# A gated mix of attention and a gated feed-forward: the first eight key tiles in one round, sixteen scores among the last projection units, and the first loads in another order

## The chip, the core and the metric

The kernel runs on one core of one Trainium2 chip. The metric is the device time of the whole launch in microseconds (us). Three runs of the kernel before gave 1299.35, 1300.30 and 1300.72 us, median 1300.3 us. Everything is float32 at the interface; most matmuls take operands that are split into a high part in the matrix format (`fp32r`) and a low part that holds the rest, so that one float32 product becomes two or three matmuls.

## The reference

`x` has 2048 tokens of width 448. Two blocks read it and their outputs are mixed per token:

```python
q, k, v = split(x @ wqkv)                      # 16 heads of 28
a = softmax(q @ k.T * 28 ** -0.5) @ v @ wo     # attention over all 2048 keys
gate, up = x @ W_gate, x @ W_up                # 448 -> 1792 each
b = (gate * (gate > 0) * up) @ W_down          # ReGLU
g = sigmoid((x * gate_w).sum(-1))
out = g * a + (1 - g) * b
```

## The kernel before, in words

The order of the instructions on every engine is written out by hand; nothing is moved by a scheduler. TensorE (PE) carries four kinds of work, and the kernel interleaves them so that PE always has one that is ready.

**Projections** (first stage). Token blocks `tb` of 512. One `qk(tb, c)` unit is 11 matmuls of 512 columns (`TERMS`: the high and low products of the four 128-row chunks of `x`, the last one packed), gives 128 rows of q and k, which ScalarE (ACT) and VectorE (DVE) split into a high and a low half in a tile `st`, and GpSimd (POOL) sends to the DRAM tensor `qk_d`. One `vproj(tb, t)` unit is 11 matmuls of 450 columns. `split_first` (line 219) splits the first weights and the first `x` chunk by chunk, as they arrive; `load_x` (line 233) issues the loads of `x` on SP's queue, and the first block's chunks 0 and 1 as one transfer each, its chunks 2 and 3 as one transfer together.

**Attention** of a head needs, for each of its 16 key tiles of 128, four *scores* (`s`, line 174: one matmul of 512 columns, then an Exp on ACT), and then a *pv* product of 8 records per key tile (`po`, line 486). Before that, the maximum of each query's scores is found by *smax* (`m` or `sm`, line 148: two matmuls of 512 columns into a two-bank PSUM tile, then a reduction on DVE, line 150); two such PSUM tiles exist, so the third smax waits for the first one's reduction. The scores have two PSUM tiles as well. `load_k(h)` and `load_q(h)` (lines 128, 132) fetch a head's K and Q from `qk_d`: four transfers each onto 28 partitions.

**The feature half-tiles** of the feed-forward: 56 feature tiles i, each with a gate half and an up half; half k is `(i, half) = divmod(k, 2)`. A half is 11 matmuls `gu` (`x`, line 451). Its weights are fetched by `fetch_f` (line 423), split by `split_f` (ACT the high part, POOL the low one), and its result goes through `relu` (ACT) or `spill_h` (DVE, then POOL's transfer to DRAM). The 56 tiles are four token blocks of 14. At the end of each block the last up half (half 27, 55 or 83) frees the four chunks of the `X` tile one after the other, and `gu_mm` (line 452) issues on SP, right behind the last matmul that reads a chunk, two transfers that load the next block's chunk into the same place. The following half (28, 56, 84) reads them.

**Rounds.** After the projections, the list `ROUNDS` says what happens between two pv products. A round is a string: `s` a score, `m` an smax, `x` one matmul of the round's halves in order, `h` the last matmuls of the last two halves as a pair on the two halves of the array. A LONG round has 32 scores, 16 smax and 3 halves; a WIDE one the same with 4 halves; LATE rounds (the last three) have no smax. The loop from line 562 runs the string, then splits the weights of the next round's halves, then does the pv of the round's key tiles. At the start of a round, and again in its middle, `small_things(u)` does what belongs to a quarter of a head: with u a multiple of four it issues `load_k(h + 2)` and `load_q(h + 2)`; with u = 1 it computes the gates.

Before, there are 34 rounds: a first one with nothing left to do (two key tiles), one with 8 scores and 4 smax (two tiles), SHORT with 16 scores, 8 smax and one half (four tiles), then 25 LONG, 3 WIDE and 3 LATE rounds of eight tiles each. Twelve scores of the first three tiles are already done among the last projection units (`EARLY`: how many units before the end each is placed). The WIDE rounds start with halves 28, 56 and 84: half 27 is the last one of a LONG round, and the pv product lies between it and half 28. The same holds for 55 and 83.

**The tail.** 100 halves are done in the rounds; the remaining 6 tiles run as `gate_up` between the `down` products, then come the rest of `down` and the output projection `wout` (line 644). The list `todo` (line 718) fixes the order; `before(i, ...)` puts `spread`, `normalise`, `fetch_o` and `wout` ahead of a given `down`, and `split_o` (ACT, then POOL) is put ahead of a given `down` and of the `gate_up` just before it, if there is one.

SP's queue is in order: a load that waits holds back all loads behind it. The loads' completion semaphores are eight, used in turn, and the ninth load waits until the first has landed.

Of the kernel before, what the change touches and what calls it, by code (L numbers as in the profile page):

```python
# [8 lines left out]
F32 = mybir.dt.float32  # L9
F32R = mybir.dt.float32r  # L10
# [8 lines left out]
P = 128  # L19
# [7 lines left out]
NF = F // P  # L27
NB = 4
TB = 512
# [3 lines left out]
NQ = 2 * D // P  # L33
WARM = 9

EARLY = (5, 5, 4, 4, 4, 3, 3, 3, 2, 2, 1, 1)


LEAD = 24

SHORT = "smsxxsmsxsmsxmsxsmsxxsmsxsmsxxsmsxs"


LONG = "mxsmsxxxxxsmsxsmsxxsmsxsmsxxsmxxsmsxsxxsmsxxsxsmxsxsmsxxsmsxsmsxxsmsxsxxsmsmxssh"
WIDE = "sxxmxmxxsxxmsxxsxsmxxssxmxmxsxxsxxsxsmsxxsmxssxxxsmsxxsxmsxmsxsxmsxsmxsxsxxsmsxxsmsmsxxsxsh"

LATE = "ssxxxssxxxssxxxssxx" * 2 + "ssxxxssxxxssxxssxx" * 2 + "h"

ROUNDS = [("ssssssss", 0), ("smssmssmsmss", 0), (SHORT, 1)] + [(LONG, 3)] * 9 + ([(WIDE, 4)] + [(LONG, 3)] * 8) * 2
ROUNDS += [(WIDE, 4)] + [(LATE, 4)] * 3  # L50
NP = 9


# [10 lines left out]
def gated_mix_kernel(ctx, tc, x, wq, wo, wgu, wd, out):  # L64
    nc = tc.nc
# [7 lines left out]
    def f32(ap):  # L73
        return ap.bitcast(F32)
# [35 lines left out]
    vp = stk.enter_context(tc.tile_pool(name="vp", bufs=1))  # L110
# [9 lines left out]
    def q_slot(name):  # L120
        return vp.tile([P, 4, TB], F32R, name=name, tag="Q", bufs=3)
# [4 lines left out]
    Q = {}  # L126

    def load_k(h):
        for r in range(4):
            nc.sync.dma_start(f32(K[h % 3])[DH * r:DH * (r + 1)], qk_d[r % 2, 2 * DH * h:2 * DH * h + DH, :])  # L130

    def load_q(h):
        Q[h] = q_slot(f"Q_{h}").rearrange("p j t -> p (j t)")
        for r in range(4):
            nc.sync.dma_start(f32(Q[h])[DH * r:DH * (r + 1)], qk_d[r // 2, 2 * DH * h + DH:2 * DH * (h + 1), :])
# [55 lines left out]
    def xf(tb, b):  # L191
        return X[tb][b // 4][:, b % 4]


    with tc.tile_pool(name="qkv", bufs=1) as pa:
        W = pa.tile([P, 7, 2 * D + VC], F32R, name="W")
# [36 lines left out]
        def load_x(tb):  # L233
            r = []
            for c in range(0, 4, 2):
                xr = pa.tile([P, 2, TB], F32, name=f"xr_{tb}_{c}", tag="stg", bufs=3)
                for a, b in ((c, c + 1), (c + 1, c + 2)) if tb + c == 0 else ((c, c + 2),):
                    nc.sync.dma_start(xr[:, a - c:b - c], x[:, a:b, tb * TB:(tb + 1) * TB])
                if tb + c == 0:
                    load_first(nc.sync, 2, 4)  # L240
                r.append((c, c + 2, xr))
            return r
# [28 lines left out]

        outs = [K[2].rearrange("p (a r t) -> p a r t", a=2, r=2)[:, a] for a in range(2)]
        sent = [0]
        late_outs = []

        def st_tile(tb, c):

            k = sent[0]
            sent[0] += 1
            if k < 15 and k % 5 > 2:  # L280
                return outs[k % 5 - 3]
            if c == NQ - 1 and tb < 2:
                if tb == 1:
                    late_outs.append(q_slot("st_last"))
                return late_outs[0][:, 2 * tb:2 * tb + 2]
            return pa.tile([P, 2, TB], F32R, name=f"st_{tb}_{c}", tag="st", bufs=3)

        def qk(tb, c, terms=TERMS, among=()):
# [25 lines left out]
        def load_first(queue, a, b):  # L314
            queue.dma_start(w0[0][:, a:b], wq[:, a:b, w0[1]:w0[2]])
# [54 lines left out]
        mixed = units[:2]  # L370
# [6 lines left out]
        for n, (f, *a) in enumerate(mixed):  # L377
            if n == 0:
                split_w(*w5)
            if n == 6:  # L380
                load_k(1)
                load_q(1)
            if n == 8:
                split_w(*w3)
            if n == 13:

                nc.gpsimd.memset(f32(K[2])[96:128], -1.0)
            if n in spills:
                spill_x(*spills[n])

            among, ends = [], m
            while n >= first and m < (n + 1 - first) * ahead / (len(mixed) - first):
                among.append((smax, m))
                m += 1
            news = [(scores, *divmod(k, NB)) for k, back in enumerate(EARLY) if back == len(mixed) - n]
            for k, c in enumerate(news):
                among.insert(2 * k + 1, c)
            f(*a, among=among)
            if ends < 2 * NK <= m:
                smax_end(0)  # L400
# [9 lines left out]

    fe = ctx.enter_context(tc.tile_pool(name="fe", bufs=1, side="right"))
    att = stk.enter_context(tc.tile_pool(name="att", bufs=1))
    WR, WS, HK = {}, {}, {}


    done = sum(n for _, n in ROUNDS) // 2
    SECOND = {sum(n for _, n in ROUNDS[:r + 1]) - 1 for r in range(len(ROUNDS)) if "h" in ROUNDS[r][0]}
    SECOND |= set(range(2 * done + 1, 2 * NB * NF, 2))

    def lane(k):  # L420
        return slice(64 * k, 64 * k + 64)

    def fetch_f(i):
        WR[i] = fe.tile([P, 2, 4, P], F32, name=f"wgr_{i}", tag="wgr", bufs=2)
        nc.sync.dma_start(WR[i], wgu[i % NF])

    def split_f(i, high, low, part=(0, 1)):

        if part[0] == 0:
            WS[i] = fe.tile([P, 2, 7, P], F32R, name=f"wg_{i}", tag="wg", bufs=2)  # L430
        w, wr = WS[i], WR[i]
        for s in part:
            high(w[:, s, 0:3], wr[:, s, 0:3])
            low(w[:, s, 3:6], wr[:, s, 0:3], w[:, s, 0:3])
        if part[-1] == 1:
            high(w[:, :, 6], wr[:, :, 3])
            for s in range(2):
                rows = lane(1 - (2 * i + s in SECOND))
                low(w[rows, s, 6], wr[rows, s, 3], w[rows, s, 6])
            del WR[i]  # L440
# [18 lines left out]
    def relu(i, ps, late=False):  # L459
        RL[i] = fe.tile([P, TB], F32, name=f"rl_{i}", tag="rl", bufs=2)  # L460
        if late:
            nc.vector.tensor_scalar_max(RL[i], ps, 0.0)
        else:
            nc.scalar.activation(RL[i], ps, AF.Relu)
# [4 lines left out]
    def spill_h(i, ps):  # L469
        h = fe.tile([P, TB], F32, name=f"h_{i}", tag="h", bufs=2)  # L470
        hidden(i, ps, h)
        h_d[i] = dram.tile([P, TB], F32, name=f"h_d_{i}")
        nc.gpsimd.dma_start(h_d[i], h)  # L473
# [80 lines left out]
        if h and q == 2:  # L554
            normalise(h - 1)

    fetch_f(0)
    fetch_f(1)
    load_k(2)
    load_q(2)  # L560
    wor = None
    for r, (order, nu) in enumerate(ROUNDS):
        ni = order.count("s") // NB
        late = order == LATE
        todo = list(range(nxt, nxt + nu))
        nxt += nu
        small_things(i0 // 4)
        if m % (2 * NK) == 0 and i0 <= NI - LEAD:
            smax_end(m // (2 * NK) - 1)
        if late and wor is None:  # L570
            wor = load_wo()

        passes = [(*divmod(k, 2), n) for k in todo for n in range(NT - ("h" in order and k >= nxt - 2))]
        units = []
        ns = 0
        for o in order:
            if o == "x" and not passes:
                continue
            if o == "s":
                i, j = i0 + 1 + ns // NB, ns % NB  # L580
                if ns == 4 * NB:
                    small_things(i0 // 4 + 1)
                if len(EARLY) <= i * NB + j < NI * NB and not late:
                    scores(i, j)
                elif late and i < NI and j % 2 == 0:
                    scores_pair(i, j)
                ns += 1
            elif o == "m":
                smax(m)
                m += 1  # L590
            elif o == "x":
                i, half, n = passes.pop(0)
                if n == 0:
                    ps = (ps_s if late else ps_x)(f"gu_{i}_{half}")
                    units.append((i, half, ps))
                gu_mm(units[-1][2], i, half, n)
                if n == NT - 1:
                    i, half, ps = units.pop()
                    spill_h(i, ps) if half else relu(i, ps, late)
            elif o == "h":  # L600
                for i, half, ps in units:
                    gu_mm(ps, i, half, NT - 1)
                for i, half, ps in units:
                    spill_h(i, ps) if half else relu(i, ps, late)
        assert not passes, (r, passes)

        ready = nxt + (ROUNDS[r + 1][1] if r + 1 < len(ROUNDS) else 2)
        ready += ready % 2
        while parts < ready:
            split_f(parts // 2, dve_high if late else act_high, pool_low, (parts % 2,))  # L610
            parts += 1
            if parts % 2 == 0:
                fetch_f(parts // 2 + 1)
        pv(i0, ni, late)
        i0 += ni
        if late and i0 == NI:
            split_wo(wor)
# [113 lines left out]
    for tb, load, split, at in ((0, 2, (3, 4), (4, 5, 6, 7)), (1, 5, (7, 9), (10, 11, 14, 14)), (2, 21, (23, 25), (28,) * 4),  # L731
                                (3, 35, (37, 39), (42,) * 4)):
        before(load, (fetch_o, tb))
        for k, i in enumerate(split):
            n = todo.index((down, i))
# [53 lines left out]
```

## Time and profile before

| | |
|---|---|
| median of 3 runs | 1300.3 us |
| the profiled execution's own time | 1300.88 us, of which the span shown is 1298.7 us |
| PE busy | 1292.3 us |
| DVE, ACT, POOL busy | 816.9, 763.4, 363.9 us |
| granted TensorE clock | 1.0 |

The profile is one execution. Times in it count from the start of the span. `L451` is line 451 of the kernel before. A view of groups or of the timeline names the engine, the line, the tiles as out<-in and the shapes; `[0.20 <-DVE mx L150]` says that the engine stood idle for 0.20 us before it, and what ended that. PEld is the loading of weights, which runs beside the matmuls. A matmul's own duration overlaps with the next one's; the distance between starts is what counts.

### The profile page before, as it was taken

How to read it: one execution, taken by the hardware profiler on the slowest of the kernel's cores; microseconds unless marked ns; L12 is line 12 of the kernel's file. 1: busy time of each engine (PE TensorE's matmuls, PEld its weight loads, DVE VectorE, ACT ScalarE, POOL GpSimd, SP SyncE). 2: the span in 40 equal slices, each digit the busy share in tenths (PEclk: the TensorE clock that was granted, in tenths of full speed). 3: DMA queues.
4: the chain of work that ended last, by engine and by line, in shares of the span. 5: the costliest groups of instructions: out<-in, count | busy, mean ns of one | idle time of the engine just before them, and what ended most of it. 6: DMA issues, size and time to landing. Idle time of an engine off the chain costs nothing.

```text
span 1298.7 us, 17695 instructions
## 1 busy us (share of the span) xinstructions
PE 1292.3 (100%) x6685; PEld 899.0 (69%) x6685; DVE 816.9 (63%) x855; ACT 763.4 (59%) x1387; POOL 363.9 (28%) x547
## 2 busy tenths in 40 slices
PE   9999999999999999999999999999999999999998
PEld 6888666666666666666666666666666566899997
DVE  5578766777767667776677677767676224553332
ACT  5312676677777676766667677777776664322121
POOL 3222123222222232223223222222223444541020
PEclk9999999999999999999999999999999999999999
DMA  9835525142343613141527243241422233734432
GB/s 311 282 156 227 160 69 114 55 109 71 78 95 91 171 57 98 49 98 58 137 68 174 59 92 83 71 91 56 99 84 87 95 96 119 255 91 157 132 110 79
DMA packets 53548, 148.85 MB, mean 115 GB/s; under 512 B 10008, under 2 KB 17112, under 8 KB 48856
## 3 DMA queue, kind: packets, MB, share of 16 engines
q1 hardware_dynamic: 36104, 98.34, 29.0%
q0 software_dynamic: 16928, 48.93, 10.4%
q8 instruction: 52, 0.85, 0.3%
q10 hardware_dynamic: 432, 0.46, 0.1%
q14 instruction: 32, 0.26, 0.1%
HBM read 102.06 MB, written 46.02 MB: 114 GB/s over the span
## 4 chain that ended last, share of the span: by engine, by line
PE 97%; DMA 1%; DVE 1%; ACT 0%; POOL 0%; issue 0%; SPq 0%; POOLq 0%; ACTq 0%
PE gu L451 22%; PE sm L148 18%; PE po L486 17%; PE s L174 17%; PE acc L690 11%; PE qk L291 5%; PE wo L644 3%; PE v L301 3%; PE s L185 2%; DMA ls<-os 1%; POOL wg L95 0%; DMA xr<-x 0%; PE mt L158 0%; ACT wg L86 0%; DVE mx L150 0%
## 5 line engine op out<-in xcount | busy, mean ns | idle before, releaser
L150 DVE TENSOR_REDUCE mx<-sm 128x1 f32<-128x1024 f32 x512 | 614.2, 1221 | 103.5 <-PE sm L148 103.0
L176 ACT ACTIVATE P<-s 128x512 f32<-128x512 f32 x724 | 415.3, 598 | 158.9 <-PE s L174 117.3
L451 PE MATMUL gu<-X,wg 128*128 128x512 f32 (+1 forms) x1232 | 389.0, 402 | 0.0
L174 PE MATMUL s<-Q,K 114*128 114x512 f32 x932 | 369.3, 402 | 0.1
L148 PE MATMUL sm<-K,Q 112*128 112x512 f32 x1024 | 324.6, 398 | 0.4 <-DVE mx L150 0.4
L451 PEld LDWEIGHTS gu<-X,wg 128*128 128x128 f32 (+1 forms) x1232 | 226.2, 189 | 55.5 <-issue 11.1
L174 PEld LDWEIGHTS s<-Q,K 114*128 114x128 f32 x932 | 175.2, 188 | 92.5 <-ACT P L176 50.4
L148 PEld LDWEIGHTS sm<-K,Q 112*128 112x128 f32 x1024 | 191.9, 190 | 46.2 <-issue 10.1
L486 PE MATMUL po<-P,V 128*32 128x512 f32 x1600 | 181.4, 594 | 0.0
L473 POOL DMA_DIRECT2D h_d<-h x56 | 31.5, 563 | 486.8 <-DVE h L467 443.8
L95 POOL TENSOR_TENSOR wg<-wgr,wg 128x384 fp32r<-128x384 f32 x204 | 146.8, 736 | 23.4 <-issue 10.2
L176 ACT ACTIVATE V<-s 128x512 f32<-128x512 f32 x208 | 119.6, 598 | 42.1 <-PE s L174 30.4
L690 PE MATMUL acc<-WD,hh 128*128 128x448 f32 x672 | 141.3, 368 | 0.0
L690 PEld LDWEIGHTS acc<-WD,hh 128*128 128x128 f32 x672 | 125.7, 188 | 13.5 <-issue 1.0
L486 PEld LDWEIGHTS po<-P,V 128*32 128x32 f32 x1600 | 49.3, 110 | 110.5 <-issue 109.5
L86 ACT ACTIVATE hh<-hr 128x512 fp32r<-128x512 f32 x56 | 35.4, 631 | 125.4 <-PE acc L690 120.4
L92 DVE TENSOR_TENSOR hh<-hr,hh 128x512 fp32r<-128x512 f32 x56 | 44.6, 796 | 65.4 <-ACT hh L86 65.4
L291 PE MATMUL qk<-X,W 128*128 128x512 f32 x308 | 79.2, 396 | 1.2 <-ACT X L86 0.8
L291 PEld LDWEIGHTS qk<-X,W 128*128 128x128 f32 x308 | 57.7, 189 | 17.2 <-ACT X L86 2.1
L492 DVE TENSOR_TENSOR os<-po,os 128x512 f32<-128x512 f32 x18 | 12.4, 692 | 88.3 <-PE po L486 82.4
L86 ACT ACTIVATE wg<-wgr 128x384 fp32r<-128x384 f32 x153 | 61.7, 492 | 2.3 <-DMA wgr<-wgu 2.3
L92 DVE TENSOR_TENSOR mh<-mr,mh 16x128 fp32r<-16x128 f32 x16 | 5.4, 337 | 85.8 <-ACT mh L162 85.6
(72 smaller groups left out, 762.4 us busy)
## 6 DMA issues: line engine op xcount, KB each, us to landing
wgr<-wgu SPq DMA_DIRECT2D x56, 512.0 KB
K<-qk_d SPq DMA_DIRECT2D x64, 224.0 KB
Q<-qk_d SPq DMA_DIRECT2D x64, 224.0 KB
h_d<-h POOLq DMA_DIRECT2D x56, 256.0 KB, 2.3
hr<-h_d SPq DMA_DIRECT2D x56, 256.0 KB
qk_d<-st POOLq DMA_DIRECT2D x20, 512.0 KB, 3.8
x_d<-X POOLq DMA_DIRECT2D x6, 1024.0 KB, 5.1
X<-x_d SPq DMA_DIRECT2D x24, 256.0 KB
```

What stands on the lines that cost most here:

```text
L86: nc.scalar.activation(dst, src, AF.Copy)
L92: nc.vector.tensor_tensor(dst, src, f32(high), op=OP.subtract)
L95: nc.gpsimd.tensor_tensor(dst, src, f32(high), op=OP.subtract)
L148: nc.tensor.matmul(ps[:, c, :], Q[h][:GD, u * P:(u + 1) * P], K[h % 3][:GD, k0:k0 + TB], start=True, stop=True)
L150: nc.vector.tensor_reduce(MX[h][:, 2 * u + half:2 * u + half + 1], ps, axis=AX.XY, op=OP.max)
L174: nc.tensor.matmul(ps, K[h % 3][:GD + 2, kt * P:(kt + 1) * P], Q[h][:GD + 2, j * TB:(j + 1) * TB], start=True, stop=True)
L176: nc.scalar.activation(PT[i][:, j], ps, AF.Exp, scale=SCALE)
L291: nc.tensor.matmul(ps, W[:, a, c * P:(c + 1) * P], xf(tb, b), start=(n == 0), stop=(n == NT - 1))
L301: nc.tensor.matmul(ps[:, :VC], xf(tb, b)[:, t * P:(t + 1) * P], W[:, a, 2 * D:], start=(n == 0), stop=(n == NT - 1))
L451: nc.tensor.matmul(ps, WS[i][rows, s, a], xf(i // NF, b)[rows], start=(n == 0), stop=(n == NT - 1))
L486: nc.tensor.matmul(po[32 * j:32 * j + 32], V[:, h // 4 % 2, i % NK, h % 4], p[:, j], start=(i == i0), stop=(i == i0 + ni - 1))
L690: nc.tensor.matmul(ACC[i // NF][t][:, :D], HH[i][:, a, t * P:(t + 1) * P], WD[:, f, b], start=(f == 0 and n == 0), stop=(f == NF - 1 and n ...
```

## The change

- `EARLY` has 16 entries: all four scores of the first four key tiles (tile 0 to 3) are done among the last projection units, four more than before, all of them in the last two units.
- The three short rounds become one round `FIRST` of eight key tiles: 20 scores (the first twelve letters `s` fall on scores already done), 12 smax and two halves, the two of feature tile 0. One pv product of eight tiles follows, where before there were three of two, two and four tiles.
- The weights of feature tile 0 are fetched earlier, six units before the end of the projections, into one half of a tile `pair` that takes a Q slot; its first half is split right behind the last unit, the second at the new letter `u` in the round. `u` also issues the loads of head 2's K and Q and of tile 2's weights. The other half of `pair` holds the last unit's `st`; the last unit but two uses an ordinary `st` tile.
- The rounds after that: 6 LONG, then three times (WIDE, 6 LONG), WIDE, 3 LATE. So there are 32 rounds, 24 LONG and 4 WIDE, and 102 halves in them. A half k now falls into another place of its round: half 27, 55 and 83 are each the *first* half of a LONG round (rounds 9, 18 and 27 counted from 0), and 28, 56 and 84 the second of the same round. The tail has 5 tiles.
- In the first loads, chunks 2 and 3 of the first block of `x` are two transfers instead of one, with the second pair of the first weights still between chunk 1 and chunk 2.

```diff
-EARLY = (5, 5, 4, 4, 4, 3, 3, 3, 2, 2, 1, 1)
+EARLY = (5, 5, 4, 4, 4, 3, 3, 3, 2, 2, 2, 2, 1, 1, 1, 1)
...
-SHORT = "smsxxsmsxsmsxmsxsmsxxsmsxsmsxxsmsxs"
+FIRST = "s" * 12 + "smssmxsmxsxsmxuxsmxsxsxmsxxsmxsxmsxxsmxsxsmxsxxmsxsxmsx"
...
-ROUNDS = [("ssssssss", 0), ("smssmssmsmss", 0), (SHORT, 1)] + [(LONG, 3)] * 9 + ([(WIDE, 4)] + [(LONG, 3)] * 8) * 2
-ROUNDS += [(WIDE, 4)] + [(LATE, 4)] * 3
+ROUNDS = [(FIRST, 2)] + [(LONG, 3)] * 6 + ([(WIDE, 4)] + [(LONG, 3)] * 6) * 3 + [(WIDE, 4)] + [(LATE, 4)] * 3
...
+    WR, WS, HK, pair = {}, {}, {}, []
+
+    def fetch_f(i):
+
+        if i == 0:
+            pair.append(vp.tile([P, 4, TB], F32, name="pair", tag="Q", bufs=3))
+            WR[i] = pair[0][:, :2].rearrange("p s (c f) -> p s c f", c=4)
+        else:
+            WR[i] = fe.tile([P, 2, 4, P], F32, name=f"wgr_{i}", tag="wgr", bufs=2)
+        nc.sync.dma_start(WR[i], wgu[i % NF])
...
-                for a, b in ((c, c + 1), (c + 1, c + 2)) if tb + c == 0 else ((c, c + 2),):
+                for a, b in ((c, c + 1), (c + 1, c + 2)) if tb == 0 else ((c, c + 2),):
...
-            if c == NQ - 1 and tb < 2:
-                if tb == 1:
-                    late_outs.append(q_slot("st_last"))
-                return late_outs[0][:, 2 * tb:2 * tb + 2]
+            if c == NQ - 1 and tb == 0:
+                return pair[0][:, 2:].bitcast(F32R)
...
+            if n == len(mixed) - 6:
+                fetch_f(0)
...
-    fetch_f(0)
+    split_f(0, act_high, pool_low, (0,))
     fetch_f(1)
-    load_k(2)
-    load_q(2)
...
+            elif o == "u":
+                split_f(0, act_high, pool_low, (1,))
+                load_k(2)
+                load_q(2)
+                fetch_f(2)
+                parts = 2
```

More of the change, by code (lines that the diff above doesn't have):

```diff
@@ L273, in gated_mix_kernel @@
         sent = [0]
-        late_outs = []
         def st_tile(tb, c):
@@ L412, in gated_mix_kernel @@
     att = stk.enter_context(tc.tile_pool(name="att", bufs=1))
-    WR, WS, HK = {}, {}, {}
     done = sum(n for _, n in ROUNDS) // 2
@@ L421, in lane @@
         return slice(64 * k, 64 * k + 64)
-    def fetch_f(i):
-        WR[i] = fe.tile([P, 2, 4, P], F32, name=f"wgr_{i}", tag="wgr", bufs=2)
-        nc.sync.dma_start(WR[i], wgu[i % NF])
     def split_f(i, high, low, part=(0, 1)):
```

## The prediction

> **What bounds the kernel.** I read the page first (busy shares, the chain that ended last), then the chain in order of time, then the timeline of each engine where the change acts: the start, the end of the projections, one LONG round, the block boundary, the tail.
>
> ```profile
> PE 1292.3 (100%) x6685; PEld 899.0 (69%) x6685; DVE 816.9 (63%) x855; ACT 763.4 (59%) x1387; POOL 363.9 (28%) x547
> PE 97%; DMA 1%; DVE 1%; ACT 0%; POOL 0%; issue 0%; SPq 0%; POOLq 0%; ACTq 0%
> 11.02 28.04 PE qk L291 x120
> 399.37 7.00 PE po L486 x64
> 429.39 7.00 PE po L486 x64
> 461.78 7.00 PE po L486 x64
> 1109.55 5.11 PE gu L451 x22
> ```
>
> PE is the bound from 11 us to the end, so only three things can move the time: PE's own work, the short waits at stage changes, and a new wait that PE runs into. The chain gives the prices: a 512-column matmul every 28.04/120 = 0.234 us there and 5.11/22 = 0.232 in the tail (0.23 below), a LONG round 429.39 - 399.37 = 30.02, a WIDE one 461.78 - 429.39 = 32.39, a tail tile 5.11 us.
>
> **Part 1, the first loads.**
>
> ```profile
> 7.63 0.63 ACT L86 ACTIVATE X<-xr 128x512 fp32r<-128x512 f32 x1 [0.92 <-DMA xr<-x]
> 8.96 1.22 ACT L86 ACTIVATE W<-wr 128x336 fp32r<-128x336 f32 x4
> 9.43 0.69 DVE L92 TENSOR_TENSOR X<-xr,X 128x512 fp32r<-128x512 f32 x1
> 10.04 1.42 DVE L92 TENSOR_TENSOR W<-wr,W 128x336 fp32r<-128x336 f32 x4
> 11.02 27.60 PEld L291 LDWEIGHTS qk<-X,W 128*128 128x128 f32 x120 [0.54 <-DVE W L92]
> 6.00:8.00 2.00, 1.48 (x5) 0.67 (x4) 1.22 (x3) 0.96 (x3) 0.93 (x5) 1.00 1.02 343
> ```
>
> ACT waits 0.92 us for chunks 2 and 3 together. Chunk 2 alone would land about 0.7 us sooner (half of 512 KB at the 343 GB/s that the last row, the stretch from 6 to 8 us, gives in its last column). ACT and DVE then run the chain chunk 2, chunk 3, next weights earlier; DVE's low parts of the next weights, which PE waits for until 11.02, follow the last chunk without a gap, so they move by as much, unless those weights land later than ACT's 8.96. One more issue on SP costs 0.45 us of a queue that is ahead of its data. Behind 11.02 PE has no gap for 27.6 us. I take -0.6 (ends 0 and -0.75).
>
> **Part 2, end of the projections and FIRST.**
>
> ```profile
> 135.83 0.79 PE L301 MATMUL v<-W,X 128*128 128x450 f32 x3
> 143.09 1.92 PE L486 MATMUL po<-P,V 128*32 128x512 f32 x16
> 154.88 0.73 PE L148 MATMUL sm<-K,Q 112*128 112x512 f32 x2 [0.20 <-DVE mx L150]
> 166.19 0.71 PE L148 MATMUL sm<-K,Q 112*128 112x512 f32 x2
> 143.69 0.59 ACT L86 ACTIVATE st_last<-qk 128x512 fp32r<-128x512 f32 x1
> 145.30 0.72 POOL L296 DMA_DIRECT2D qk_d<-st_last  x1 [3.17 <-DVE st_last L92]
> 152.39 0.78 DVE L406 TENSOR_SCALAR e<-e 128x16 f32<-128x16 f32 x1
> 149.51 1.09 ACT L176 ACTIVATE P<-s 128x512 f32<-128x512 f32 x2 [0.26 <-PE s L174]
> 153.62 8.16 DVE L150 TENSOR_REDUCE mx<-sm 128x1 f32<-128x1024 f32 x7
> ```
>
> From the last unit but one (135.83) to the first LONG round (166.19) PE takes 30.34 us. Its work there, at 0.23 (0.2045 for the 450-column ones), is 28 scores 6.4, 15 smax 6.9, two units 4.8, one half 2.5 and three pv products 7.0, in all 27.6: 2.7 us are lost at the three changes to pv and back and in waits for reductions. FIRST has the same and one half more, 30.1. I walked through its string with ACT at 0.5 to 0.6 us per Exp (two take 1.09) and DVE at 8.16/7 = 1.2 per reduction. Three places wait: the third score (its PSUM tile's Exp stands behind the last `st` and the new split on ACT: 1.2 us); the second `x` (its low part stands on POOL behind the transfer that waits for DVE, as at 145.30 now: covered by the smax); and the sixth smax (DVE has the gates, 1.2 us, between the third and fourth reduction: 0.8 us), together 1.85. Weights of tile 2 come behind Q of head 2, which waits for `pair`; ACT meets that wait only while the pv product runs, 7 us of cover. So 32.0 against 30.3: +1.6, ends +0.7 (a LONG round's own loss) and +3.5.
>
> **Part 3, rounds and tail.** One LONG becomes WIDE: +2.37. The tail loses a tile: -5.11. But the tile covered something: `wout` of block 0 stands behind `down` 3 and one `gate_up` now, and directly behind `down` 3 after.
>
> ```profile
> 1088.30 10.68 PE L451 MATMUL gu<-X,wg 128*128 128x512 f32 x44
> 1123.46 1.05 ACT L86 ACTIVATE on<-or 128x1024 fp32r<-128x1024 f32 x1
> 1125.76 2.42 POOL L95 TENSOR_TENSOR on<-or,on 128x1024 fp32r<-128x1024 f32 x1
> 1130.07 2.50 PE L644 MATMUL wo<-WO,on 128*128 128x448 f32 x11
> ```
>
> The second low part of `on` is ready 39.9 us after the tail's start; PE needs it with the tenth matmul of `wout`, now at 43.6. After, the same ACT and POOL order puts it at 39.9 again, and PE is there at 36.7 + 1.8 = 38.5: a wait of 1.4 (ends 0 and 2.5).
>
> **Part 4, the block boundary, which decides.** Now each boundary's eight `X` loads run under the pv product. After, half 27 (55, 83) is first in a LONG round and half 28 (56, 84) follows at once. Rows of the LONG round that starts at 678.87, and the transfers around it (slices of 0.5 us from 676):
>
> ```profile
> 678.87 0.73 PE L148 MATMUL sm<-K,Q 112*128 112x512 f32 x2
> 680.60 1.33 PE L451 MATMUL gu<-X,wg 128*128 128x512 f32 x5
> 686.49 0.62 PE L451 MATMUL gu<-X,wg 128*128 128x512 f32 x2
> 677.49 1.65 SPq L130 DMA_DIRECT2D K<-qk_d  x4
> 679.25 3.09 SPq L135 DMA_DIRECT2D Q<-qk_d  x4
> DMA  0000947999889468999569899439979854410002
> SPq L455 <- DMA K<-qk_d: 1.9, 1, 1.9
> 422.17 7.60 SPq L455 DMA_DIRECT2D X<-x_d  x8
> GB/s 0 0 0 0 0 0 106 172 193 332 225 74 180 172 356 283 82 147 303 324 160 209 152 279 340 361 246 57 0 0 0 66 205 262 393 123 0 41 147 172
> ```
>
> Call the start T. The third `x`, the last reader of chunk 0, is the second of the five at 680.60, so chunk 0 is free at about T + 2.4. The next half's first matmul is the second of the pair at 686.49: T + 7.85. The cover is 5.4 us. Alone, the first chunk needs some 3.3: issued at 422.17, its 0.5 MB are through by 425.5 (last row, slices of 0.5 us from 420). So the boundaries in rounds 9 and 27 should stay hidden, with 1 to 2 us to spare.
>
> Round 18 starts with u = 36, a multiple of four, so head 11's eight K and Q loads stand on SP just ahead of the `X` loads. The same head quarter starts the round shown: there K and Q are issued from T - 1.4 to T + 3.5, and the DMA engines stay busy with them until 694, T + 15. In the changed program each `X` load also waits for the completion of one of those eight (SP already waits so for 1.9 us in this round). Are `X` loads served behind all K and Q data, or beside it?
>
> ```profile
> 156.13 1.59 SPq L135 DMA_DIRECT2D Q<-qk_d  x4
> 157.82 9.93 SPq L425 DMA_DIRECT2D wgr<-wgu  x2
> DMA  9987998678500100000139599987963000000093
> ```
>
> Here a 512 KB weight load was issued at 157.82 right behind four Q loads. Transfers run until 163.5 (slices from 158): nothing else was issued, so this load took over 5 us, against 3.3 for the 0.5 MB of the first `X` chunk above. That speaks for one after the other. The Trainium skill, "DMA: Bandwidth & Descriptors", section "Queues, rings and completion order", has each DMA engine consume one queue's descriptors in ring order; by it the `X` data comes last, and the row agrees.
>
> Then chunk 0's first half lands at T + 15 + 0.8 (256 KB at 330 GB/s) + 0.4 = T + 16.2, and PE waits 16.2 - 7.85 = 8.3 us. The other chunks follow 1.6 us apart, faster than the half asks for them. Lower end: only the issue waits count; K and Q landing one after the other until T + 15, the last chunk lands some 3.4 us later, T + 18.5, and is asked for at T + 14.3: 4.2 us. Upper end 9.5.
>
> A PE that stood idle also starts slowly in this trace: after the start its weight loads, one per matmul, come 0.43 us apart, against 0.23 later (first and last of seven rows).
>
> ```profile
> 1.59 0.15 PEld L328 LDWEIGHTS <-warm 128*128 128x128 bf16 x1 [0.28 <-issue]
> 4.15 0.15 PEld L328 LDWEIGHTS <-warm 128*128 128x128 bf16 x1 [0.28 <-issue]
> ```
>
> These span 2.6 us, the slow stretch may have lasted until the last warm-up matmul. No row shows PE idle so long later, so the price lies between 0 and (1 - 0.23/0.43) x 4 = 1.9; I take 1.7, since eight idle microseconds resemble the start more than the gaps under 1 us. The Trainium skill, "TensorE: Matmul & The Clock Gate", Part 1, halves the clock after an idle window of about 3.4 us and lifts it after a busy one; by that alone the price would be an estimated 1.7.
>
> **The sum.** -0.6 + 1.6 + 2.4 - 5.1 + 1.4 + 8.3 + 1.7 = +9.7 us on the profiled execution's 1300.9. That execution lies 0.6 above the median, 1300.3; I forecast 1310.0.
>
> **Rivals.** (a) As forecast, but PE resumes at full speed: 1308.3. For it: no row shows a slow matmul after the start, and the clock column (1.00 in the row of 6 to 8 us) is 1.00 in every stretch, the start among them, so that it can't tell. (b) `X` is served beside K and Q, and only the issue waits: 4.2 instead of 8.3, mostly in waits too short to slow PE: 1300.3 - 0.3 + 4.2 = 1304.2. Against it: the load at 157.82. (c) Not slower: the `X` loads of round 18 land by T + 7.85. It decides if K and Q are through by about T + 4, which needs them four times faster than the row shows; then all else sums to -0.3: 1300.0. (d) The other two boundaries are late too, if a chunk needs over 5.4 us from issue to landing there; the halves' transfers and `h_d` share the engines. Two more at 2 us each, a chunk of 7.4 us: 1314.0.
>
> **How the numbers follow.** Forecast 0.48, (a) 0.18, (b) 0.12, (c) 0.14, (d) 0.08. The range leaves out (c) and the far part of (d): 1303.5 to 1313. A change of 0.2% (2.6 us) is about what a measurement tells from none. All cases but (c) are slower by more: 0.86. Within (c), part 2 at its lower end and no wait for `on` would give -2.7 or a little more: faster 0.05, same 0.09.
>
> **What would show it.** In the profile after: one PE idle of about 8 us before a `gu` matmul in round 18, near 690 us (round 1 starts near 167, then 15 LONG and 2 WIDE rounds, and 7.85), put down to an `X` load or to SP; none over 1 us at the two other boundaries; matmul starts 0.43 apart for 3 to 4 us behind it; PE's real start near 10.4; FIRST's pv product starting near 160; a wait of 1 to 2 us in the first `wout`. Wrong it would be if PE runs through round 18 without a gap, or if FIRST loses more than 4 us to ACT or DVE.

## The result, and the profile after

The changed kernel takes 1309.36 us (median of 6 runs, 1307.86 to 1310.79), the kernel before beside it 1300.44 us: ratio 1.0066, 95% interval 1.0052 to 1.0081, 0.66% slower. The forecast was 1310.0, +9.7 us; it came out at +8.9 by the medians. The profiled execution took 1310.79 us, its span is 1309.0 (before: 1300.88 and 1298.7), so the account below explains 10.3 us of span.

First the page: the busy shares, the clock column, and two groups whose last column is PE's idle time and what ended it. Kernel after:

```profile
PE 1291.8 (99%) x6685; PEld 900.6 (69%) x6685; DVE 814.0 (62%) x849; ACT 761.9 (58%) x1387; POOL 366.6 (28%) x551
PEclk9999999999999999999998999999999999999999
L455 PE MATMUL gu<-X,wg 128*128 128x512 f32 (+1 forms) x1232 | 392.7, 402 | 7.9 <-DMA X<-x_d 7.9
L148 PE MATMUL sm<-K,Q 112*128 112x512 f32 x1024 | 324.0, 397 | 1.6 <-DMA Q<-qk_d 1.6
```

PE's matmuls are as many as before (6685), and it is busy as long. What is new is idle time, and one slice of 40 in which the clock isn't full. Now the chain of work, in order of time, kernel after (pv products; start, duration):

```profile
404.57 7.01 PE po L490 x64
434.52 7.01 PE po L490 x64
554.37 7.01 PE po L490 x64
586.79 7.00 PE po L490 x64
676.63 7.01 PE po L490 x64
688.86 10.56 DMA X<-x_d
716.42 7.01 PE po L490 x64
1094.97 7.00 PE po L490 x64
```

Two starts differ by a round: LONG 434.52 - 404.57 = 29.95, WIDE 586.79 - 554.37 = 32.42, and round 18 takes 716.42 - 676.63 = 39.79, 9.84 more than a LONG round. The chain holds an `X` load there: issued at 688.86, landed 10.56 us later. PE and SP in that round (timeline):

```profile
682.19 1.65 SPq L130 DMA_DIRECT2D K<-qk_d  x4
683.95 3.07 SPq L135 DMA_DIRECT2D Q<-qk_d  x4
688.86 10.48 SPq L459 DMA_DIRECT2D X<-x_d  x8
691.20 0.39 PE L455 MATMUL gu<-X,wg 128*128 128x512 f32 x1
699.46 0.80 PE L455 MATMUL gu<-X,wg 128*128 128x512 f32 x1 [7.87 <-DMA X<-x_d]
700.05 0.63 PE L174 MATMUL s<-Q,K 114*128 114x512 f32 x1
700.48 1.05 PE L148 MATMUL sm<-K,Q 112*128 112x512 f32 x2
701.33 1.29 PE L455 MATMUL gu<-X,wg 128*128 128x512 f32 x2
702.41 0.61 PE L174 MATMUL s<-Q,K 114*128 114x512 f32 x1
702.84 0.65 PE L148 MATMUL sm<-K,Q 112*128 112x512 f32 x2
```

PE stops for 8 us at the first matmul that reads the new `X`. Behind the stop seven matmuls take 702.84 - 699.46 = 3.38 us, 0.48 each, and the next ones 0.23 or 0.24 again: 3.38 - 7 x 0.232 = 1.76 us lost. Stretches of 3 us around it (length, then PE, PEld, DVE, ACT and POOL busy, then the granted clock, the share of the DMA engines, GB/s):

```profile
685.00:688.00 3.00, 3.00 (x15) 2.33 (x14) 2.31 (x3) 1.98 (x4) 0.44 (x1) 1.00 0.87 131
694.00:697.00 3.00, 0.00 (x0) 0.00 (x0) 0.00 (x0) 0.00 (x0) 0.00 (x0) 0.84 0.95 180
697.00:700.00 3.00, 0.54 (x1) 0.50 (x2) 0.00 (x0) 0.00 (x0) 0.00 (x0) 0.50 1.05 277
700.00:703.00 3.00, 3.00 (x8) 1.99 (x7) 1.23 (x1) 0.60 (x1) 0.00 (x0) 0.52 0.93 358
703.00:706.00 3.00, 3.00 (x15) 2.25 (x14) 1.80 (x2) 2.63 (x5) 0.00 (x0) 1.00 0.22 83
```

A mean of 0.84 over 3 us is 0.96 us at one half, 0.52 is 2.88: the granted clock is at one half from 696.0 to 702.9, that is from about 4.5 us into the stop to 3.4 us behind it, and full again after. The DMA engines are busy all the time from 685 to 703 (a share of 0.87 or more in every stretch of 3 us).

Smaller places of the timeline, kernel after: the first smax, the last unit but one, the third score of FIRST, the first LONG round, the first `wout`.

```profile
53.09 0.70 PE L148 MATMUL sm<-K,Q 112*128 112x512 f32 x2 [1.59 <-DMA Q<-qk_d]
136.93 0.58 PE L309 MATMUL v<-W,X 128*128 128x450 f32 x2
147.36 0.50 PE L174 MATMUL s<-Q,K 114*128 114x512 f32 x1 [0.88 <-ACT P L176]
169.38 0.28 PE L158 MATMUL mt<-ident,m 128*16 128x128 f32 x1
1138.38 1.99 PE L652 MATMUL wo<-WO,on 128*128 128x448 f32 x9
1141.69 0.68 PE L652 MATMUL wo<-WO,on 128*128 128x448 f32 x2 [1.33 <-POOL on L95]
```

The 10.3 us of span are then: start to the last unit but one +1.1 (136.93 against 135.83); that unit to the first LONG round +2.1; round 18 +9.8; one LONG round turned WIDE +2.4; the other LONG rounds, 29.95 to 29.96 here against 30.02, -1.4; the tail from the last pv product on -3.3 (1309.0 - 1094.97 against 1298.7 - 1081.36); some -0.4 left over in the rounds, since one pair of LONG rounds in the trace before, from 884.45, had taken 60.53 us in place of 60.04.

### The profile page after: what moved, and what is told of

It is laid out like the page before. It is cut to its first block, busy times and chain, and to the rows that moved or that the text cites. A ratio compares the mean times of both kernels' runs of the same rounds, so it can differ in the third digit from the quotient of the medians.

```text
span 1309.0 us, 17699 instructions
## 1 busy us (share of the span) xinstructions
PE 1291.8 (99%) x6685; PEld 900.6 (69%) x6685; DVE 814.0 (62%) x849; ACT 761.9 (58%) x1387; POOL 366.6 (28%) x551
## 4 chain that ended last, share of the span: by engine, by line
PE 95%; DMA 2%; issue 1%; POOL 0%; SPq 0%; ACT 0%; DVE 0%; ACTq 0%; POOLq 0%; DVEq 0%
PE gu L455 22%; PE sm L148 18%; PE po L490 17%; PE s L174 17%; PE acc L698 10%; PE qk L299 4%; PE wo L652 3%; PE v L309 2%; PE s L185 2%; DMA Q<-qk_d 1%; DMA X<-x_d 1%; DMA wr<-wq 0%; DMA qk_d<-K 0%; PE mt L158 0%; POOL on L95 0%
```

## The experiments

The theory: one stall makes the result, because `X` stands behind head 11's K and Q, and the rest of the change is worth next to nothing. Runs with the same time before were made together on one chip, with the kernel before beside them; "vs before" is the ratio with its 95% interval.

| run | median us | before us | vs before |
|---|---|---|---|
| e1_kq_behind_x | 1301.09 | 1301.03 | 1.0000 (0.9992 to 1.0009) |
| e2_kq_on_pool | 1310.88 | 1301.03 | 1.0073 (1.0060 to 1.0085) |
| e3_busy_wait | 1310.25 | 1301.03 | 1.0072 (1.0056 to 1.0088) |
| e4_one_load | 1311.06 | 1301.03 | 1.0085 (1.0072 to 1.0098) |
| e5_e1_one_load | 1300.01 | 1299.84 | 1.0000 (0.9992 to 1.0009) |
| e6_e1_wout_later | 1297.75 | 1299.84 | 0.9988 (0.9979 to 0.9996) |
| e7_all | 1298.33 | 1299.84 | 0.9988 (0.9979 to 0.9997) |
| e8_again (the change itself) | 1309.49 | 1299.84 | 1.0077 (1.0063 to 1.0090) |
| e9_first | 1296.75 | 1299.46 | 0.9982 (0.9973 to 0.9991) |
| e10_busy_36 | 1307.95 | 1299.46 | 1.0069 (1.0055 to 1.0083) |
| e11_q_behind_x | 1301.90 | 1299.46 | 1.0015 (1.0006 to 1.0024) |
| e12_all | 1297.22 | 1299.46 | 0.9984 (0.9975 to 0.9993) |

### K and Q behind X

```diff
-        if q == 0 and h and h + 2 < H:
+        if q == 0 and h and h + 2 < H and u != 36:
...
                 gu_mm(units[-1][2], i, half, n)
+                if (i, half, n) == (2 * NF - 1, 1, NT - 1):
+                    load_k(11)
+                    load_q(11)
```

> The changed kernel (1309.4 us) with one edit: in round 18 the eight loads of head 11's K and Q are issued behind the eight X loads instead of ahead of them. Theory (X is late because it stands behind K and Q in one queue): PE's wait of 7.9 us for X goes, and with it the slow matmuls behind it, 1.7 us: 1299.7. Rival (the cover of 5.4 us is too short for X whatever stands ahead of it): a wait of 2 us or more stays there, 1302 or more. If K and Q in turn come too late, the first smax of round 19 waits for Q.

Measured: no different from the kernel before, some 9 us below the changed one. The SP rows of this kernel's timeline, and two pv products around round 18 from its chain:

```profile
686.21 6.18 SPq L459 DMA_DIRECT2D X<-x_d  x8
692.44 1.69 SPq L130 DMA_DIRECT2D K<-qk_d  x4
694.23 3.36 SPq L135 DMA_DIRECT2D Q<-qk_d  x4
```

```profile
677.10 7.00 PE po L490 x64
707.07 7.00 PE po L490 x64
```

Round 18 takes 29.97 us, an ordinary LONG round, PE waits for no `X`, and the next round doesn't wait for K or Q. Swapping two groups of eight loads takes the whole cost away. So 5.4 us of cover are enough for `X` by itself, and the other parts of the change add up to nothing that can be measured: the interval of the ratio is 0.09%, 1.2 us, to either side.

### Half of the loads ahead

```diff
-            load_q(h + 2)
+            if u != 36:
+                load_q(h + 2)
...
+                if (i, half, n) == (2 * NF - 1, 1, NT - 1):
+                    load_q(11)
```

> The changed kernel (1309.5 us) with only head 11's four Q loads behind X; the four K loads stay ahead of it. Theory (X comes one after the other behind what was issued ahead of it, 1.2 us for each load onto 28 partitions after the first): K is through four loads earlier, so the wait is 8.0 - 4 x 1.2 = 3.2 us or less, too short for much of the slow stretch: 1309.5 - 4.8 - 1.7 = 1303. Rival (any load ahead of X costs the completion wait in full): no better than 1307.

```profile
PE gu L455 <- DMA X<-x_d: 2.5, 2, 1.5
```

Total, times and longest of the waits of that kernel: 1.5 and 1.0 us, below the 3.2 that the theory gave as the most; the clock stays at 1.0. By the medians the kernel is 2.4 us over the kernel before (1.9 by the ratio). Its runs fall into two groups, five from 1299.66 to 1300.84 and six from 1301.90 to 1303.83, and the trace is of the slower one; no trace shows what `X` does in the faster. The price goes with the number of loads ahead: eight 7.9 us, four 2.5, none 0. By the Trainium skill, "DMA: Bandwidth & Descriptors", section "Queues, rings and completion order", each DMA engine works through one queue's descriptors in ring order; the first wait of each run agrees. The second wait here, of 1.0 us at 698.24, is not explained by it: `X` moves at 380 GB/s from 690 to 695, and its last chunk still counts as landed only 3 us later. That stays open.

### K and Q on another queue

`load_k` and `load_q` take the queue as an argument here; their own lines are left out.

```diff
-            load_k(h + 2)
-            load_q(h + 2)
+            queue = nc.gpsimd if u == 36 else nc.sync
+            load_k(h + 2, queue)
+            load_q(h + 2, queue)
```

> The changed kernel (1309.4 us) with head 11's K and Q loads issued on POOL's queue instead of SP's, at the same place in the program. They move the same bytes at the same time. Theory (order within a queue decides): the X loads of round 18 are issued without waiting for K's and Q's completion and served beside them, so that a 256 KB X load takes about twice its time alone, some 6 us instead of 10.5: PE's wait is 0 to 2.5 us, 1299.7 to 1303.5. Rival (the DMA engines are simply full, in whatever queue): the wait stays near 8 us, 1309.

The theory's figure fell here: 1310.88, as slow as the change. The waits (total, times, longest), PE's timeline and one stretch of 3 us of this kernel:

```profile
PE gu L455 <- DMA X<-x_d: 6.1, 3, 3.4
```

```profile
695.77 0.80 PE L455 MATMUL gu<-X,wg 128*128 128x512 f32 x1 [3.37 <-DMA X<-x_d]
699.88 0.80 PE L455 MATMUL gu<-X,wg 128*128 128x512 f32 x1 [2.46 <-DMA X<-x_d]
```

```profile
697.00:700.00 3.00, 0.54 (x2) 0.12 (x1) 0.00 (x0) 0.60 (x1) 0.00 (x0) 0.50 0.83 245
```

`X` does get a place beside K and Q: there is no single stop of 8 us but waits of 0.2, 3.4 and 2.5 at its chunks. But the engines now carry both at once, every chunk comes late, and the clock falls to one half as well and stays there longer, from 695.1 to 705.3. Round 18 takes 39.92 us, 10.0 more than a LONG round, of which 6.1 are the waits. So the place in the queue isn't all that counts: 1.8 MB that PE reads only in the next round, some 22 us later, move in the same time as `X`. Nor do SP's own waits make the cost: in the kernel after, SP stands 9.3 us in eight waits until K and Q loads have landed before it issues the `X` loads, here in none. The same section of the Trainium skill has each engine take turns between the queues that have work for it; by that `X` is beside, not ahead, and the three short waits fit.

### Matmuls in the wait

```diff
                     units.append((i, half, ps))
+                    if (i, half) == (2 * NF, 0):
+                        for c in range(26):
+                            nc.tensor.matmul(ps, Q[9][:GD, :P], K[0][:GD, :TB], start=True, stop=True)
```

> The changed kernel (1309.4 us) with 26 additional matmuls of 512 columns (of head 9's Q and K, their result overwritten), 6 us of PE's work at 0.23, placed right ahead of the first matmul that waits for X in round 18. Theory (PE runs slowly behind the wait because it stood idle): PE now stands idle for only some 2 us, the matmuls behind it come 0.23 us apart from the start, the wait's end stays where it is: 1307.7. Rival (they are slow because X is arriving, or the clock has another reason): the same 1309.4.

The six runs fall into two groups, 1306.8 to 1308.5, around the theory's 1307.7, and 1312.0 to 1313.8, above the rival's 1309.4. The trace is of the first group: clock 1.0 throughout, and behind the shortened wait the matmuls come at the full rate. So a second run with 36 of them:

> As e3_busy_wait with 36 additional matmuls instead of 26, 8.4 us of work in a wait of 8.0. Three of that kernel's executions were 1 to 3 us below the changed kernel and three were 3 to 4 us above it, with a lower mean clock. Theory (in those three X came later, so that PE stood idle behind the additional matmuls and slowed down after all): with no idle time left no execution is above 1310; all lie near 1309.4 + 0.4 - 1.7 = 1308.1, clock 1.0. Rival (the additional matmuls themselves bring the lower clock): executions near 1313 with a clock of 0.997 are there again, or more of them.

Five runs from 1307.51 to 1309.01, mean clock 0.999 to 1.0. PE's timeline of e10_busy_36 at the same place:

```profile
689.39 8.33 PE L600 MATMUL gu<-K,Q 112*128 112x512 f32 x36
697.83 0.50 PE L455 MATMUL gu<-X,wg 128*128 128x512 f32 x1
698.16 0.40 PE L174 MATMUL s<-Q,K 114*128 114x512 f32 x1
698.40 0.63 PE L148 MATMUL sm<-K,Q 112*128 112x512 f32 x2
698.87 0.39 PE L455 MATMUL gu<-X,wg 128*128 128x512 f32 x1
```

Four matmuls behind the wait take 698.87 - 697.83 = 1.04 us, 0.26 each, where the changed kernel needs 0.48. One wait for a later chunk is left, 0.69 us at 699.95, and the clock stays at 1.0. `X` arrives in both kernels, so its arrival isn't what slows the matmuls; that PE stood idle is. The rival, that the additional matmuls bring the lower clock, is out: ten more of them brought none. That `X` came later still in the slow three of e3_busy_wait fits, but no trace of these exists; it stays open. The time agrees with the forecast of 1308.1; against e8_again (another set of runs) the ratios' intervals overlap, so the 1.7 us rest on the traces. The Trainium skill, "TensorE: Matmul & The Clock Gate", Part 1, has the clock halved after an idle window of about 3.4 us and full again after a busy one: the row of half clock in the kernel after, which begins some 4.5 us into the stop and ends 3.4 us behind it, agrees. The second trace of the same kernel, e8_again, does not (PE's stop, and the stretch in which the clock falls):

```profile
698.22 0.80 PE L455 MATMUL gu<-X,wg 128*128 128x512 f32 x1 [8.37 <-DMA X<-x_d]
689.00:692.00 3.00, 0.85 (x4) 0.31 (x2) 2.24 (x3) 1.15 (x3) 0.46 (x1) 0.94 1.10 165
```

The stop begins at 698.22 - 8.37 = 689.85. A mean of 0.94 over 3 us is 0.36 us at one half, so the clock falls at 691.6, 1.8 us into the stop, and by the same reckoning it is full again at 701.9. In e2_kq_on_pool it falls 2.7 us into a stop of 3.4. So a stop need not hold an idle window of 3.4 us for the clock to fall; the measurement decides.

### The first loads

```diff
-                for a, b in ((c, c + 1), (c + 1, c + 2)) if tb == 0 else ((c, c + 2),):
+                for a, b in ((c, c + 1), (c + 1, c + 2)) if tb + c == 0 else ((c, c + 2),):
```

> The changed kernel (1309.4 us) with the first block's chunks 2 and 3 loaded as one transfer again, as in the kernel before. Theory (the split costs, because it turns the order of the transfers behind it, so that Q of head 0 lands 2 us later): PE's projections start 0.7 us later, at 11.0, but the first smax no longer waits 1.6 us for Q and starts near 52.1 instead of 53.1: 1308.3. Rival (the split gains what the prediction said, and Q's delay has another cause): 1310.0.

> Head 11's K and Q behind X as in e1_kq_behind_x (1301.1 us, which has little scatter), and the first block's chunks 2 and 3 loaded as one transfer again. Theory (the split moves PE's start 0.7 us forward in every execution, and the first smax waits for Q in some of them only): 1301.1 + 0.2 to 0.7 = 1301.3 to 1301.8, PE's wait for the first X near 1.1. Rival (the split costs, since Q is late because of it): 1300.0, and no wait of the first smax.

The first smax in four kernels: e8_again and e1_kq_behind_x (split), e4_one_load and e5_e1_one_load (one load):

```profile
51.54 0.67 PE L148 MATMUL sm<-K,Q 112*128 112x512 f32 x2
```

```profile
53.58 0.70 PE L148 MATMUL sm<-K,Q 112*128 112x512 f32 x2 [1.74 <-issue]
```

```profile
52.34 0.63 PE L148 MATMUL sm<-K,Q 112*128 112x512 f32 x2
```

```profile
52.82 0.70 PE L148 MATMUL sm<-K,Q 112*128 112x512 f32 x2 [0.45 <-issue]
```

Up to there e8_again and e1_kq_behind_x are the same program, as is the changed kernel. The wait comes and goes between executions of one program, and with one load it can come too. The theory of e4_one_load, that the split costs 1 us by delaying Q, is wrong: without the wait the split is 0.8 us ahead (51.54 against 52.34), as forecast; with it, the kernel after (53.09) is 0.8 behind. Nine traces have the split and this smax at its old place: six of them show no wait and start it at 51.25 to 51.68, three wait 0.45 to 1.74 us. In the times e4_one_load is no faster than e8_again and e5_e1_one_load no different from e1_kq_behind_x: the times show no difference, and each ratio is known only to 1.2 us or more. The traces show one step of the delay. Some projection units use a tile `K` as their `st`, whose earlier contents may still be on their way to `qk_d`; in the kernel after and in e1_kq_behind_x ACT waits 2.9 and 2.8 us for such a transfer to land and writes the tile at 31.72 and 31.97, in e8_again it waits for PE only and writes it at 30.93. The first K load follows at 38.15, 38.22 and 36.16. e11_q_behind_x has that wait of ACT too (2.6 us) and its smax does not wait, so it takes more than this step; why the transfer lands later in some executions stays open.

### wout later, FIRST in another order

```diff
-    for tb, load, split, at in ((0, 2, (3, 4), (4, 5, 6, 7)), (1, 5, (7, 9), (10, 11, 14, 14)), (2, 21, (23, 25), (28,) * 4),
+    for tb, load, split, at in ((0, 2, (3, 4), (5, 6, 7, 8)), (1, 5, (7, 9), (10, 11, 14, 14)), (2, 21, (23, 25), (28,) * 4),
```

> As e1_kq_behind_x (1301.1 us), and the four output products of block 0 one down product later each, behind down 4, 5, 6 and 7 instead of 3, 4, 5 and 6. Theory (the tile taken from the tail had covered the second low part of on): PE's wait of 1.3 us before the tenth matmul of wout goes and nothing takes its place: 1299.8. Rival (the wait is handed on to the next down or to the end): 1301.1.

PE's wait for `on` is gone from the waits and nothing took its place: 2.1 us below the kernel before by the medians, 1.6 by the ratio (0.5 to 2.7), where the theory said 1.2 below. e7_all adds two edits, the first smax one unit later and FIRST's beginning (`last` holds the transfer of the last `st`, which `qk` leaves to this place):

```diff
-FIRST = "s" * 12 + "smssmxsmxsxsmxuxsmxsxsxmsxxsmxsxmsxxsmxsxsmxsxxmsxsxmsx"
+FIRST = "s" * 12 + "smsmxssxmsxsmxuxsmxsxsxmsxxsmxsxmsxxsmxsxsmxsxxmsxsxmsx"
...
     split_f(0, act_high, pool_low, (0,))
+    last[0]()
...
-        m, first, ahead = 0, 8, 2 * LEAD + 4
+        m, first, ahead = 0, 9, 2 * LEAD + 4
```

> As e6_e1_wout_later with two more edits. The first smax begins one projection unit later (2.5 us), so that it waits for Q in no execution (up to 1.7 us in some). In FIRST the second smax and the first feature matmul come ahead of the third score, and POOL makes the low part of tile 0's weights before it sends the last st: the third score's wait (0.9 us) and the second feature matmul's (0.25) go. If all three waits go and nothing takes their place: 1299.8 - 0.5 - 1.0 = 1298.3. Rival (DVE's reductions, now denser, set FIRST's pace): 1299.8.

It was no better than e6_e1_wout_later, and its timeline shows why:

```profile
107.64 0.27 PE L158 MATMUL mt<-ident,m 128*16 128x128 f32 x1 [1.63 <-DVE m L153]
```

Neither theory had this: with the later start head 0's last smax ends a unit exactly, so the transpose of the maxima stands directly behind it and waits for DVE. Two runs take that apart: FIRST's edits alone, and all with the transpose a unit later (`if ends <= 2 * NK < m`).

> As e6_e1_wout_later (2.1 us below the kernel before on one chip), and of e7_all only the edits in FIRST: the second smax and the first feature matmul ahead of the third score, POOL's low part ahead of its transfer of the last st. Theory (e7_all lost on its later first smax what it won in FIRST): the third score's wait falls from 0.9 to 0.2 us, the transpose of head 0's maxima waits for nothing, 0.7 to 0.9 us less than e6_e1_wout_later, 2.8 to 3.0 below before. Rival (DVE sets FIRST's pace): 2.1 below before.

> As e9_first, with the first smax one projection unit later as in e7_all, but the transpose of head 0's maxima one unit later too, so that it doesn't stand right behind the last reduction it needs. Theory (the first smax waits for Q in some executions, the transpose then for nothing): the same as e9_first or up to 0.5 us less. Rival (a denser DVE hands the wait on): more than e9_first by 0.5 or above.

e9_first has no wait for `s` or `mt` any more and the lowest median: 1296.75 against 1299.46, ratio 0.9982 (0.9973 to 0.9991), so some 0.2% faster than the kernel before and 0.9% than the change. It is 2.7 us below the kernel before by the medians, where the theory said 2.8 to 3.0 and the rival 2.1; the interval overlaps that of e6_e1_wout_later, so what FIRST's edits gain rests on the traces. e12_all, 0.5 above it, is no faster: the later smax buys nothing.

## Why the prediction was right

**Part 4, the boundary, +8.3 and +1.7**: right in place, mechanism and size. The wait is 7.9 us (8.4 in e8_again) in place of 8.3, it ends at T + 15.9 in place of T + 16.2 (T is 683.57), the round costs 9.84 in place of 10.0, the slow stretch 1.76. e1_kq_behind_x and e11_q_behind_x confirm the order, e10_busy_36 that idleness is what slows PE. Rival (a), full speed after the stop, is out by the 0.48 us per matmul. Rival (c), `X` in time, was out by the trace, and (d) too: the waits after hold one `X` wait only, not three.

**Rival (b) was priced wrongly.** It took service beside K and Q as worth half the wait, 1304.2, with the waits too short to slow PE. e2_kq_on_pool makes that case: 1310.88. For the time, the argument that had to decide between one after the other and beside each other decided nothing: the engines are full until about 703 in the kernel after and until about 702 in e2_kq_on_pool.

**Part 1, -0.6**: PE's real start, the first weight load behind its last early wait, came as forecast, at 10.30 in place of 11.02 (forecast 10.4; 10.45 in e8_again). The sentence "Behind 11.02 PE has no gap for 27.6 us" was true and too short: the gap came later, at the first smax, whose Q is loaded behind a chain of transfers and lands with little to spare. In the profiled execution the part cost 1.1; in others the first smax comes as much earlier as was forecast.

**Part 2, +1.6**: measured 169.38 - 136.93 = 32.45 against 32.0. FIRST's pv product starts at 162.38, not near 160, by the errors of this part and of part 1. The waits were taken too large: the third score loses 1.0 (its start is 1.28 behind the second one's, where 0.24 is usual), not 1.2, and the sixth smax, priced at 0.8, nothing. The second feature matmul, which was to be covered, loses some 0.3 (at 149.28, to the low part of its weights from POOL). That is 1.3 us in place of 1.85. The working's own prices, 1.2 and 0.8, add up to 2.0 and not to 1.85, and 166.19 - 135.83 is 30.36, not 30.34; neither changes the forecast by more than 0.2. The work was taken too small. From the third score to the pv product (length of the stretch, PE busy, its matmuls with those that reach into it, clock, DMA share, GB/s; kernel after):

```profile
147.36:162.38 15.02, 14.99 (x63) 1.00 0.81 193
```

FIRST's string has 18 scores, 11 smax of two and 22 feature matmuls there, 62 in all: 0.242 each, 0.238 without the second feature matmul's 0.3, where the working had 0.23. With the like ahead of the third score that is the remaining 1.0 us.

**Part 3**: WIDE for LONG +2.4 as forecast, `on` 1.33 for 1.4, the tail -3.3 for -3.7.

**What no term had.** The LONG rounds are 0.06 us shorter than in the trace before, together 1.4 us. It isn't the change: two kernels with the same rounds show both values, e1_kq_behind_x first and e6_e1_wout_later below it (chain of work):

```profile
435.02 7.00 PE po L490 x64
464.96 7.00 PE po L490 x64
```

```profile
433.53 7.00 PE po L490 x64
463.54 7.00 PE po L490 x64
```

29.94 and 30.01. So two traces of the same rounds may differ by some 1.5 us in PE's pace alone, and two of one program by 1.5 to 2 us at the first smax. The errors of the sum, +1.7 in part 1, +0.5 in part 2, +0.4 in the tail, -0.2 in round 18 and the -1.8 that had no term, nearly cancel: that the forecast lies within 0.7 us of the median is in part luck. What carries it is the stall with its slow stretch, 9.8 us of 10.3.

## What to carry to other kernels

Where a change shifts a loop's phase, look at what each block boundary now meets: here a load needed within 5 us had to be issued ahead of loads needed in 20, and another queue did not replace that order, since the engines then carried both. PE came back at half the clock from the stops of 7.9, 8.4 and 3.4 us, which cost 1.8 us more behind one stop of 8 and 3.9 in the kernel with two stops of 3.4 and 2.5; behind stops of 1.5 and 1.0 us (e11_q_behind_x) the clock was full. Price every other part against what two executions of one program differ by, here 1 to 2 us, and undo the parts one by one before keeping any: without its stall the change was worth nothing, and with two waits of about 1 us taken out it was a gain of 0.2%.

## What was not expected of the hardware

- Loads onto 28 partitions keep the DMA engines as busy as the `X` loads do and move half as much: 131 to 180 GB/s at 0.87 to 0.95 of the engines' time while K and Q pass, 358 GB/s at 0.93 while `X` does.
- The granted clock fell to one half 1.8 us (e8_again), 2.7 us (e2_kq_on_pool) and 4.5 us (the kernel after) into a stop of PE, and stayed there for some 7 to 10 us.
- PE's pace has two values between executions at a granted clock of 1.0: the mean of a LONG round is 29.95 to 29.96 us in nine traces and 30.02 in five (the kernel before, e4_one_load, e5_e1_one_load, e6_e1_wout_later, e7_all). Two chips show both values. The cause is open.
